# Attention and a rational feed-forward block on one core: a stored instruction order in place of a list scheduler, and six early loads on ScalarE's queue

## The chip, the core and the metric

The kernel runs on one core of a Trainium2 chip. The core has TensorE (PE in the profile), VectorE (DVE), ScalarE (ACT), GpSimd (POOL) and SyncE (SP), each with its own queue of instructions that it works through in order; they meet through semaphores. Loads and stores are issued on the queue of an engine (SPq or ACTq in the profile when they are) and carried out by 16 DMA engines. The metric is the device time of one execution in microseconds.

## The reference, cut to what matters

```python
q, k, v: (8, 8, 576, 64);  p: (8, 8, 32, 64);  w_in: (512, 2048);  w_out: (2048, 512);  a: (4,);  b: (2,)

def sm_attn(qq, kk, vv):
    s = scale * qq @ kk.T                   # scale = 1 / 8
    s = exp(s - max(s, -1))
    return (s / (sum(s, -1) + 1e-9)) @ vv

pp  = sm_attn(p, k, v)                      # 32 packed rows for each head
att = sm_attn(q, pp, pp)                    # 576 x 64 for each head
x = att.transpose(0, 2, 1, 3).reshape(4608, 512)
h = x @ w_in
P = a[0] + a[1]*h + a[2]*h**2 + a[3]*h**3
Q = 1 + abs(b[0])*abs(h) + abs(b[1])*h**2
out = (P / (Q + 1e-6)) @ w_out
```

The two weight matrices arrive as 64-bit floats, 8 MB each, and are turned into 32-bit floats on the chip, in integer arithmetic.

## The kernel before

**Work.** The eight batches go one after another. For each there is a generator `attention(bb)` (L614), then sixteen *units* (two halves of 288 tokens by eight chunks of 256 hidden columns). A unit is `hidden` (L880): TensorE forms h in PSUM (tile `h`), ScalarE and VectorE form the rational function from it (`Y`, `U`, `sq`, `V`), and the result becomes the tile `gh` (and `gl`, its rest). Three units later `acc_block` (L963) multiplies it by w_out into the tiles `acc`. `m_chunk` (L852) multiplies packed values by a chunk of w_in, which gives the tile `m` that `hidden` uses as weights. `remainder` (L932) does the last 64 tokens of two batches together (`at<-w,half` in the profile). The first batch is computed in plain 32-bit matmuls, with twelve of its units also plain in the second product; all later work splits each operand in two parts of shorter mantissa (`gh`/`gl`, `AH`/`AL`) and multiplies three of the four pairs.

**Start.** Before the first unit, q, k, v and p of batch 0 have to arrive, attention of batch 0 has to run, and weights have to be converted: `convert` (L495) takes a *word* (1 MB as it comes from memory), with two ScalarE operations and three on VectorE, the last of them on GpSimd for every second word. There are sixteen words. `constants` (L401) forms scaled copies of `a` and `b` and a square root of |b[1]| from `b`: a chain of twelve small VectorE operations and two on ScalarE (`Ln`, `Exp`), and four `reg_load`s that put results into ScalarE's registers, which the first `hidden` needs.

**Order.** The whole kernel is first recorded: `Planner` (L31) keeps 6793 entries (engine, operation, operands), a tiled group of matmuls being one entry. `edges` (L157) finds what must precede what. `schedule` (L192) is a list scheduler with a table of costs and latencies; `order` (L250) runs it forward and backward in turn, 5 slacks by 6 rounds, and keeps the best. The first 26 entries (loads for the start, and one GpSimd copy) are pinned: they come first on their queues in program order. `issue` (L281) then emits all entries in the order found, so each engine's queue is fixed. `idle` (L1075) puts short matmuls with a zero operand (`zero`) in front of a TensorE entry where the planner's times leave it a gap of at least 180 ns within the first 150 us.

The start's loads are recorded at L1006 to L1011, all on SyncE: two words, the last 64 rows of k (`AH<-in_k`), a third word, p (`pn`, four loads of 16 KB), k, rows of q, a fourth word, v, a fifth word and q; then in `constants` the four numbers `a` and the two numbers `b`, each broadcast over 128 partitions (`ab`).

Of the kernel before, what the change touches and what calls it, by code (L numbers as in the profile page):

```python
# [23 lines left out]
P = 128  # L24
# [4 lines left out]
S = 2.0**-40  # L29


class Planner:
# [27 lines left out]
    ROUNDS = 6  # L60
    SWITCH = 95
    SLACK = 60, 100, 150, 220, 300
# [5 lines left out]
    def __init__(self, nc):  # L68
        self.nc, self.ops, self.pinned = nc, [], 0
# [122 lines left out]
    def schedule(self, before, after, rank, back=0):  # L192

        n = len(rank)
        need = [len(x) for x in before]
        at, start, end = [0.0] * n, [0.0] * n, [0.0] * n
        soon = {e: [] for e in self.ENGINES}
        ready = {e: [] for e in self.ENGINES}
        free = dict.fromkeys(self.ENGINES, 0.0) if back else dict(self.FIRST)
        port = {"vector": 0.0, "gpsimd": 0.0}  # L200
        mode, landed, dma = None, [], 0.0
        for i in range(n):
            if not need[i]:
                heapq.heappush(soon[self.ops[i][0]], (0.0, rank[i], i))
        now = 0.0
        left = n
        while left:
            for e in self.ENGINES:
                while soon[e] and soon[e][0][0] <= now:
                    heapq.heappush(ready[e], heapq.heappop(soon[e])[1:])  # L210
                if free[e] > now or not ready[e]:
                    continue
                if e == "sync" and not back and len(landed) >= self.IN_FLIGHT and landed[-self.IN_FLIGHT] > now:
                    free[e] = landed[-self.IN_FLIGHT]
                    continue
                _, i = heapq.heappop(ready[e])
                left -= 1
                s = now
                if e == "tensor" and not back and self.modes[i] != mode:
                    s += self.SWITCH  # L220
                    mode = self.modes[i]
                if not back and self.shared[i]:
                    s = max(s, port["vector" if e == "gpsimd" else "gpsimd"])
                    port[e] = s + self.costs[i]
                start[i] = s
                end[i] = free[e] = s + self.costs[i]
                if e == "sync":
                    if back:
                        dma = max(dma, end[i]) + self.transfers[i]
                        end[i] = dma + self.DMA_START + self.DMA_END - self.DMA_ISSUE  # L230
                    else:
                        dma = max(dma, s + self.DMA_START) + self.transfers[i]
                        end[i] = dma + self.DMA_END
                        landed.append(end[i])
                for j in after[i]:
                    need[j] -= 1
                    f = self.ops[j][0]
                    way = self.WAY.get((f, e) if back else (e, f), self.PASS)
                    way += back * (way > 0)
                    at[j] = max(at[j], end[i] + way)  # L240
                    if not need[j]:
                        heapq.heappush(soon[f], (at[j], rank[j], j))
            now = min(
                t
                for e in self.ENGINES
                for t in ([free[e]] if ready[e] else [max(soon[e][0][0], free[e])] if soon[e] else [1e12])
            )
        return start, end

    def order(self):  # L250
# [7 lines left out]
        for i, x in enumerate(before):  # L258
            for j in x:
                after[j].append(i)  # L260
# [863 lines left out]
```

## Time and profile before

| what | value |
|---|---|
| three timed runs | 774.97, 776.93, 778.88 us; median 776.93 |
| the profiled execution's own time | 776.27 us |
| its span, first to last instruction | 774.5 us |
| mean granted TensorE clock | 0.990 |
| busy: PE, DVE, ACT, POOL | 740.3, 687.1, 653.0, 473.2 us |
| moved by DMA | 56.0 MB, of which 19.9 MB in the first 60 us |

The profile is of one execution, 1.8 us longer than its span and 0.66 us below the median of the timed runs. Busy times of TensorE come from modelled ends of pipelined matmuls. The profile names lines of the recorder: nearly every operation has line L291, so groups are told apart by their tiles (`h<-AH,m` is the output tile, then the inputs).

### The profile page before, as it was taken

How to read it: one execution, taken by the hardware profiler on the slowest of the kernel's cores; microseconds unless marked ns; L12 is line 12 of the kernel's file. 1: busy time of each engine (PE TensorE's matmuls, PEld its weight loads, DVE VectorE, ACT ScalarE, POOL GpSimd, SP SyncE). 2: the span in 40 equal slices, each digit the busy share in tenths (PEclk: the TensorE clock that was granted, in tenths of full speed). 3: DMA queues.
4: the chain of work that ended last, by engine and by line, in shares of the span. 5: the costliest groups of instructions: out<-in, count | busy, mean ns of one | idle time of the engine just before them, and what ended most of it. 6: DMA issues, size and time to landing. Idle time of an engine off the chain costs nothing.

```text
span 774.5 us, 14987 instructions
## 1 busy us (share of the span) xinstructions
PE 740.3 (96%) x5332; PEld 568.4 (73%) x5332; DVE 687.1 (89%) x1289; ACT 653.0 (84%) x1465; POOL 473.2 (61%) x456
## 2 busy tenths in 40 slices
PE   2779999999999999999999999999999999999997
PEld 2445554588778887778788887778788887868885
DVE  4899999998999889998999889998999889998863
ACT  5789988999887898889886898989887898898872
POOL 1143568876695557756686556755686556866663
PEclk9879999999999999999999999999999999999999
DMA  9992630204601155023701155023701141000001
GB/s 299 338 372 76 193 41 0 85 29 55 104 1 56 44 68 91 1 87 48 111 1 55 45 55 104 2 86 41 117 1 55 42 57 35 1 2 28 28 0 41
DMA packets 152171, 56.03 MB, mean 72 GB/s; under 512 B 122272, under 2 KB 141472, under 8 KB 152096
## 3 DMA queue, kind: packets, MB, share of 16 engines
q1 hardware_dynamic: 151856, 54.81, 31.0%
q8 instruction: 42, 0.69, 0.4%
q14 instruction: 33, 0.27, 0.1%
q10 hardware_dynamic: 240, 0.26, 0.1%
HBM read 45.62 MB, written 9.44 MB: 71 GB/s over the span
## 4 chain that ended last, share of the span: by engine, by line
PE 68%; DVE 16%; DMA 7%; ACT 4%; issue 2%; POOL 2%; SPq 1%; ACTq 0%; DVEq 0%; POOLq 0%
PE acc L291 35%; PE h L291 20%; PE at L291 12%; DVE Y L291 8%; DMA w<-in_moe_w_in_dram 2%; DMA m<-in_moe_w_in_dram 2%; DVE V L291 2%; DVE kx L291 2%; DVE m L291 2%; DVE small L291 2%; DMA w<-in_q_dram 1%; SPq L291 1%; ACT Y L291 1%; POOL gl L291 1%; DVE w L291 1%
## 5 line engine op out<-in xcount | busy, mean ns | idle before, releaser
L291 POOL TENSOR_TENSOR U<-U,sq 128x576 f32<-128x576 f32 x128 | 185.4, 1449 | 94.6 <-ACT sq L291 47.3
L291 PE MATMUL acc<-w,gh 128*128 128x512 f32 x736 | 235.7, 406 | 0.7 <-DVE G L291 0.4
L291 PE MATMUL h<-AH,m 128*128 128x288 f32 x1024 | 199.5, 317 | 4.0 <-DVE Y L291 3.5
L291 PEld LDWEIGHTS h<-AH,m 128*128 128x128 f32 x1024 | 161.2, 189 | 46.5 <-DVE Y L291 24.5
L291 POOL TENSOR_TENSOR gl<-Y,gh 128x512 fp32r<-128x512 f32 x116 | 150.3, 1296 | 45.0 <-ACT gh L291 22.8
L291 PEld LDWEIGHTS acc<-w,gh 128*128 128x128 f32 x736 | 132.6, 188 | 38.7 <-issue 9.1
L291 ACT ACTIVATE Y<-h,abS 128x288 f32<-128x288 f32 x256 | 127.5, 513 | 30.5 <-PE h L291 26.2
L291 PE MATMUL acc<-w,gl 128*128 128x512 f32 x384 | 149.3, 413 | 0.0
L291 DVE SCALAR_TENSOR_TENSOR Y<-Y,abS,V 128x576 f32<-128x576 f32 x128 | 103.2, 806 | 35.2 <-ACT V L291 34.9
L291 ACT ACTIVATE sq<-h 128x288 f32<-128x288 f32 x256 | 108.4, 425 | 29.0 <-PE h L291 15.7
L291 DVE TENSOR_TENSOR Y<-Y,h 128x288 f32<-128x288 f32 x256 | 111.0, 448 | 20.6 <-ACT U L291 7.6
L291 DVE SCALAR_TENSOR_TENSOR Y<-Y,abS,h 128x288 f32<-128x288 f32 x256 | 125.7, 507 | 2.2
L291 ACT ACTIVATE U<-h 128x288 f32<-128x288 f32 x256 | 101.9, 426 | 8.0 <-DVE V L291 7.0
L291 ACT ACTIVATE V<-U,one 128x576 f32<-128x576 f32 x128 | 98.7, 771 | 8.0 <-DVE Y L291 3.8
L291 DVE SCALAR_TENSOR_TENSOR V<-U,V 128x576 f32<-128x576 f32 x128 | 96.4, 753 | 0.0
L291 PE MATMUL h<-AL,m 128*128 128x288 f32 x448 | 96.3, 295 | 0.0
L291 DVE SCALAR_TENSOR_TENSOR Y<-V,Y 128x576 f32<-128x576 f32 x116 | 87.1, 751 | 1.4
L291 PEld LDWEIGHTS acc<-w,gl 128*128 128x128 f32 x384 | 71.8, 188 | 20.7 <-issue 6.8
L291 ACT ACTIVATE V<-V 128x576 f32<-128x576 f32 x128 | 85.0, 664 | 0.8
L291 ACT CAST gh<-Y 128x512 fp32r<-128x512 f32 x116 | 74.1, 638 | 7.4 <-DVE Y L291 6.9
L291 PE MATMUL acc<-half,gh 128*128 128x512 f32 x240 | 80.0, 411 | 0.0
L291 POOL COPY G<-Y 128x64 f32<-128x64 f32 x116 | 27.5, 237 | 76.7 <-DVE Y L291 70.5
(139 smaller groups left out, 1007.5 us busy)
## 6 DMA issues: line engine op xcount, KB each, us to landing
w<-in_moe_w_out_dram SPq DMA_DIRECT2D x16, 512.0 KB, 6.6
out_dram<-half SPq DMA_DIRECT2D x15, 512.0 KB, 3.0
nat<-in_k_dram SPq DMA_DIRECT2D x48, 144.0 KB, 3.8
nat<-in_q_dram SPq DMA_DIRECT2D x48, 144.0 KB, 4.3
nat<-in_v_dram SPq DMA_DIRECT2D x24, 256.0 KB, 3.4
m<-in_moe_w_in_dram SPq DMA_DIRECT2D x10, 512.0 KB, 6.9
w<-in_moe_w_in_dram SPq DMA_DIRECT2D x6, 512.0 KB, 8.7
nat<-in_k_dram SPq DMA_DIRECT2D x4, 512.0 KB, 6.4
```

The costliest lines, as they stand in the source:

```text
L291: getattr(getattr(self.nc, engine), name)(*args, **kwargs)
```

## The change

**The order.** The list scheduler and its rounds go. In their place stands a text of about 8,000 characters, `ORDER`, which unpacks to 6793 numbers, one for each recorded entry. `replay` walks through that order once with the old costs, only to get start times, which `idle` still uses.

```diff
-        after = [[] for _ in range(n)]
-        for i, x in enumerate(before):
-            for j in x:
-                after[j].append(i)
-        first = self.schedule(before, after, list(range(n)))
-        best = None
-        for slack in self.SLACK:
-            start, end = first
-            for r in range(self.ROUNDS):
-                s, e = self.schedule(after, before, [-x for x in end], slack)
...
+        low, high = np.frombuffer(zlib.decompress(base64.b85decode(ORDER)), np.uint8).reshape(2, -1).astype(int)
+        order = (np.cumsum(low + 256 * high) % 2**16).tolist()
+        place = {i: r for r, i in enumerate(order)}
+        assert sorted(order) == list(range(n)), "the order is of another program"
+        assert all(place[j] < place[i] for i in range(n) for j in before[i]), "the order breaks a dependence"
+        self.start, self.end = self.replay(order, before)
...
+    def replay(self, order, before):
+
+        start, end = [0.0] * len(order), [0.0] * len(order)
+        free, port = dict(self.FIRST), {"vector": 0.0, "gpsimd": 0.0}
+        mode, landed, dma = None, [], 0.0
+        for i in order:
+            e = self.ops[i][0]
+            s = max([free[e]] + [end[j] + self.WAY.get((self.ops[j][0], e), self.PASS) for j in before[i]])
...
+            start[i], end[i] = s, s + self.costs[i]
+            free[e] = end[i]
```

**The early loads.** `b`, the four loads of batch 0's p, and `a` move from SyncE's queue to ScalarE's and are recorded first. The GpSimd copy of p is recorded after all loads of the start. Nothing is pinned any more.

```diff
-        nc.sync.dma_start(ab[:, 0:4], a.rearrange("(o n) -> o n", o=1).broadcast_to([P, 4]))
-        nc.sync.dma_start(ab[:, 4:6], b.rearrange("(o n) -> o n", o=1).broadcast_to([P, 2]))
...
-                nc.sync.dma_start(pn[32 * j : 32 * j + 32, :, 0, :], src)
-            nc.gpsimd.tensor_copy(pn[:, :, 1, :], pn[:, :, 0, :])
+                (nc.sync if bb else nc.scalar).dma_start(pn[32 * j : 32 * j + 32, :, 0, :], src)
+            if bb:
+                nc.gpsimd.tensor_copy(pn[:, :, 1, :], pn[:, :, 0, :])
...
-    for what in (2, "r", 3, "p", "k0", "k1", "qr", 4, "rv", "v0", "v1", 5, "q0", "q1"):
+    nc.scalar.dma_start(ab[:, 4:6], b.rearrange("(o n) -> o n", o=1).broadcast_to([P, 2]))
+    load(0, "p")
+    nc.scalar.dma_start(ab[:, 0:4], a.rearrange("(o n) -> o n", o=1).broadcast_to([P, 4]))
+    for what in (2, "r", 3, "k0", "k1", "qr", 4, "rv", "v0", "v1", 5, "q0", "q1"):
...
-    nc.pin()
+    nc.gpsimd.tensor_copy(NAT[0, "p"][:, :, 1, :], NAT[0, "p"][:, :, 0, :])
```

**What the table says.** Unpacked with the two lines of `order`, and each number named by the entry that the code records under it, the table's queues begin like this (`w` is half a word of weights):

```
SP before:  w w w w, k rows, w w, p p p p, k k, q rows x2, w w, v rows x2, v v, w w, q q, b, a, ...
SP after:   w w w w, w w, k rows,          k k, q rows x2, w w, v rows x2, v v, w w, q q,       ...
ACT before: 6 operations of three words, 4 copies of kx, small, kx, 2 of a fourth word, ...
ACT after:  b, p p p p, a, reg_load x3, Ln, Exp, reg_load, 6 operations of three words, 4 copies of kx, small, kx, ...
DVE before: one, zero, 8 operations of three words, ...     (the 12 small ones of constants at places 29 to 53, counted from 0)
DVE after:  one, zero, the 12 small ones, 8 operations of three words, ...
```

On TensorE the first 69 entries, through the products of `win` for three chunks, are the same but for the place of a few transposes; after that the order differs throughout, though entries stay near their old places (on average 7.5 places away among 3352). The old order runs through `h` and `acc` in blocks of 2 to 12; the new one mixes them: it changes from `h` to `acc` or back 834 times, where the old one does so 310 times. Changes between tiled groups of small matmuls and whole ones are 146, before 152. Early on ScalarE's queue, the copies of `m` for the second chunk (entries 240 and 241) now come ahead of the conversion of the word in `w2` (272 and 273), where they came after it; the copies of `m` for the third chunk (280, 281) and the copy of `small` (328) also come earlier, by a few places each.

More of the change, by code (lines that the diff above doesn't have):

```diff
@@ L1 @@
-import heapq
-from collections import deque
+import base64
+import zlib
 from contextlib import ExitStack
@@ L190, in edges @@
         return edges
[L192 to L200, printed above, removed]
-        mode, landed, dma = None, [], 0.0
[L202 to L247, printed above, removed]
@@ new lines, in replay @@
+    def replay(self, order, before):
+        start, end = [0.0] * len(order), [0.0] * len(order)
+        free, port = dict(self.FIRST), {"vector": 0.0, "gpsimd": 0.0}
+        mode, landed, dma = None, [], 0.0
+        for i in order:
+            e = self.ops[i][0]
+            s = max([free[e]] + [end[j] + self.WAY.get((self.ops[j][0], e), self.PASS) for j in before[i]])
+            if e == "sync" and len(landed) >= self.IN_FLIGHT:
+                s = max(s, landed[-self.IN_FLIGHT])
+            if e == "tensor" and self.modes[i] != mode:
+                s, mode = s + self.SWITCH, self.modes[i]
+            if self.shared[i]:
+                s = max(s, port["vector" if e == "gpsimd" else "gpsimd"])
+                port[e] = s + self.costs[i]
+            start[i], end[i] = s, s + self.costs[i]
+            free[e] = end[i]
+            if e == "sync":
+                dma = max(dma, s + self.DMA_START) + self.transfers[i]
+                end[i] = dma + self.DMA_END
+                landed.append(end[i])
@@ L256, in order @@
         before = self.edges()
-        after = [[] for _ in range(n)]
-        for i, x in enumerate(before):
-            for j in x:
-                after[j].append(i)
-        first = self.schedule(before, after, list(range(n)))
-        best = None
-        for slack in self.SLACK:
-            start, end = first
-            for r in range(self.ROUNDS):
-                s, e = self.schedule(after, before, [-x for x in end], slack)
-                m = max(e)
-                rank = [m - x for x in e]
-                rank[: self.pinned] = range(-self.pinned, 0)
-                start, end = self.schedule(before, after, rank)
-                if best is None or max(end) < best[0]:
-                    best = self.best = max(end), start, end
-        self.end, self.start = best[0], best[1]
-        self.deps, self.t0 = dict(enumerate(before)), best[1]
-        return sorted(range(n), key=lambda i: (best[1][i], i))
-    def pin(self):
-        self.pinned = len(self.ops)
+        low, high = np.frombuffer(zlib.decompress(base64.b85decode(ORDER)), np.uint8).reshape(2, -1).astype(int)
[4 more added lines that the diff above has]
+        self.start, self.end = self.replay(order, before)
+        self.deps, self.t0, self.best = dict(enumerate(before)), self.start, (max(self.end), self.start, self.end)
+        return order
     def issue(self, idle):
```

103 lines of the change are left out of this document (100 added, 3 removed).

## The prediction

> **What bounds the kernel now.** I read the page first, then the busy time by stretches, then TensorE's waits.
>
> ```profile
> span 774.5 us, 14987 instructions
> PE 740.3 (96%) x5332; PEld 568.4 (73%) x5332; DVE 687.1 (89%) x1289; ACT 653.0 (84%) x1465; POOL 473.2 (61%) x456
> PE   2779999999999999999999999999999999999997
> DMA  9992630204601155023701155023701141000001
> ```
>
> TensorE is busy nearly everywhere except in the first three of 40 slices, and just there the DMA engines are at 9 tenths or more. The stretches, with TensorE's busy time first, then its weight loads, VectorE, ScalarE, GpSimd:
>
> ```profile
> 0.00:20.00 20.00, 4.97 (x22) 4.42 (x22) 9.72 (x10) 10.32 (x12) 3.36 (x8) 1.00 0.97 297
> 20.00:40.00 20.00, 15.19 (x244) 8.69 (x242) 16.99 (x45) 15.53 (x35) 2.43 (x1) 0.87 1.08 343
> 40.00:60.00 20.00, 15.31 (x87) 9.57 (x88) 17.39 (x28) 16.83 (x34) 8.32 (x5) 0.79 1.02 354
> 60.00:80.00 20.00, 20.00 (x167) 11.25 (x166) 19.96 (x41) 19.89 (x45) 7.73 (x5) 1.00 0.17 55
> 80.00:100.00 20.00, 19.34 (x95) 10.26 (x95) 19.77 (x37) 19.99 (x40) 14.62 (x7) 1.00 0.70 195
> 400.00:500.00 100.00, 99.84 (x750) 79.44 (x748) 90.66 (x173) 86.00 (x198) 66.42 (x66) 1.00 0.28 50
> ```
>
> From 0 to 60 us TensorE is idle for 15.03 + 4.81 + 4.69 = 24.5 us, from a span of which it is idle 34.2 (774.5 - 740.3). From 60 to 100 us TensorE, VectorE and ScalarE are full at once, and in the middle of the kernel TensorE idles 0.16 us in 100. So another order can win in the first 60 us, a little in the stretch after it, and hardly anything in the middle of the kernel unless the matmuls themselves run closer together. TensorE's waits say the same:
>
> ```profile
> PE at L291 <- DMA nat<-in_k_dram: 15.0, 1, 15.0
> PE at L291 <- ACT m L291: 4.3, 4, 1.6
> PE h L291 <- DVE Y L291: 3.5, 4, 1.8
> PE at L291 <- ACT small L291: 2.1, 1, 2.1
> ```
>
> All the waits that it names and that are over 2 us are here; the first three columns after the colon are the sum, the count and the longest.
>
> **Part 1, p and the constants leave SyncE's queue.**
>
> ```profile
> 4.74 3.40 SPq L291 DMA_DIRECT2D pn<-in_p_dram  x4
> 9.56 1.30 SPq L291 DMA_DIRECT2D nat<-in_k_dram  x2
> ab<-in_moe_b_dram SPq DMA_DIRECT2D x1, 1.0 KB, 8.8
> pn<-in_p_dram SPq DMA_DIRECT2D x4, 16.0 KB, 7.6
> out_dram<-full ACTq DMA_DIRECT2D x2, 64.0 KB, 2.5
> ```
>
> (The last three: KB each and us from issue to landing; p's is that of the first 24 us.) SyncE can issue k up to 4.8 us earlier (9.56 - 4.74). But k is queued behind six loads of 512 KB and one of 128 KB, 3.3 MB, and the stretch to 20 us has its DMA engines 0.97 busy at 297 GB/s: 3.3 MB take 11 us at that rate whenever they are issued. What goes away ahead of k is p's own 64 KB, 0.2 us at 297 GB/s, and p must still be moved by the same engines beside it. I take **-0.2**; bounds 0 and -4.8 (the whole earlier issue). The constants' two loads stood behind q and held nothing that the path waits for.
>
> **Part 2, the same six loads at the head of ScalarE's queue.** This is the price of the change. Behind them the table puts three `reg_load`s, `Ln`, `Exp` and a fourth `reg_load`, all of which need `a` or `b` landed and the small VectorE chain done; and behind these stand the six conversions of the first three words and then the copies of `kx` that attention needs. What waits for a late ScalarE is therefore all of attention.
>
> ```profile
> 0.73 1.28 ACT L365 ACT_TABLE_LOAD   x1 [0.73 <-PEq L1109]
> 5.87 1.10 ACT L291 ACTIVATE m<-m 128x1024 f32<-128x1024 f32 x1 [3.85 <-DMA m<-in_moe_w_in_dram]
> 6.87 1.10 ACT L291 ACTIVATE win<-m 128x1024 int32<-128x1024 uint32 x1
> 14.29 1.12 ACT L291 ACTIVATE win<-m 128x1024 int32<-128x1024 uint32 x1
> 16.09 0.59 ACT L291 COPY kx<-at 128x512 f32<-128x512 f32 x1 [0.67 <-PE at L291]
> 37.41 0.27 DVE L291 TENSOR_SCALAR root<-root 128x1 f32<-128x1 f32 x1
> 37.88 0.21 ACT L291 ACTIVATE root<-root 128x1 f32<-128x1 f32 x1
> 769.37 0.85 ACTq L291 DMA_DIRECT2D out_dram<-full  x2
> ```
>
> Two issues on ScalarE's queue took 0.85 us, so six take 2.6; the table load ends at 2.01, the sixth, `a`, starts at 4.1. No row shows a load on ScalarE's queue beside a full SyncE queue. Nearest is a store there at 2.5 us; as far up as it goes is `b`'s 8.8 us in the full queue; as far down, the shortest landing of p in this run:
>
> ```profile
> DMA to landing us min/median/max: 1.5/1.8/8.6
> ```
>
> So `a` lands between 5.6 and 12.9 us; with 2.5 us, at 6.6. The chain behind it is about 1.5 us of work after `b`'s part (rows in part 3) and four passages between engines; `Ln` (37.88) started 0.2 us after the end of the VectorE operation that it waits for, so I estimate 2.3 us. The first conversion then starts at 8.9 (7.9 to 15.2) in place of 5.87. Six conversions at one per 1.00 us (5.87 to 6.87) with a last of 1.12 take 6.1, ending at 15.0 (14.0 to 21.3), where the first copy of `kx` started at 16.09. At 15.0 the delay is covered, because the six took from 5.87 to 15.41 before, 3.4 us more than they need; at 21.3 attention starts 5.2 us late. I take **+0.5**, between 0 and **+5.2**, near the store's row.
>
> The Trainium skill (DMA: Bandwidth & Descriptors, "Queues, rings and completion order") says that each DMA engine goes round-robin between the queues that have work, packet by packet, so these small loads would not stand behind SyncE's backlog; by it they land near 1.5 us, the term is 0 and the sum 0.5 us lower. No run here shows it yet. The same page ("Issuing engines are not separate DMA queues") says that a second issuing engine saves issue time only; the trace, with its DMA engines 0.97 busy, agrees, as in part 1.
>
> **Part 3, the constants' chain leaves VectorE's busy stretch.**
>
> ```profile
> L291 DVE TENSOR_SCALAR root<-root x5: 113/146/267, 32.4 to 37.4; 128x1 int32<-128x1 int32 x3, 128x1 f32<-128x1 f32 x2
> L291 DVE RECIPROCAL root<-root x2: 156/156/156, 36.6 to 38.9; 128x1 f32<-128x1 f32 x2
> L291 ACT ACTIVATE root<-root x2: 213/214/216, 37.9 to 38.2; 128x1 f32<-128x1 f32 x2
> L291 DVE SCALAR_TENSOR_TENSOR root<-root x1: 214/214/214, 39.1 to 39.1; 128x1 f32<-128x1 f32 x1
> ```
>
> Five at about 0.146, two at 0.156 and one of 0.214 make 1.26; the other four (`root` from `ab`, three writes of `abS`) are as small, about 0.15 each: 1.9 us in all. They stood between 31 and 40 us, ahead of the first `h`. In the first 20 us VectorE is idle for 10.3 (20 - 9.72), so there they cost nothing unless `a` is late as in part 2. **-1.9**; bounds 0 (if TensorE then waits for something else) and -2.3 with ScalarE's two.
>
> **Part 4, the reordering from 40 to 60 us.** ScalarE's copies of `m` and `small` move ahead of word conversions: these are the waits of 4.3 and 2.1 us above. What is late next is VectorE or ScalarE themselves, which have 20 - 17.39 = 2.6 and 20 - 16.83 = 3.2 us to give in that stretch. So at most 6.4, and I take the smaller of the two, **-2.6**; bounds 0 and -6.4.
>
> **Part 5, the rest.** Two things are left on TensorE after 60 us: short matmuls that fill planned gaps, and waits of `h` for `Y` (3.5 us, above).
>
> ```profile
> L288 PE MATMUL acc<-w,zero 128*64 128x96 f32 x14 | 2.2, 264 | 0.0
> L288 PE MATMUL acc<-half,zero 128*64 128x96 f32 x6 | 0.7, 254 | 0.0
> ```
>
> Fillers are 2.9 us busy, in a stretch where VectorE is full too: **-1.0**, bounds 0 and -2.9. Of the waits, **-2.0**, bounds 0 and -3.5. The finer mixing of `h` and `acc` itself I cost at nothing, from the chain of waits:
>
> ```profile
> 149.13 1.85 PE h L291 x12
> 160.84 1.58 PE h L291 x12
> 162.42 2.09 PE acc L291 x9
> ```
>
> The 12 matmuls of `h` end at 162.42 and the 9 of `acc` start there: going from one to the other took no time. What covers it is that both operands have long been ready; the first row, 0.27 us longer for the same 12, shows a block whose cover was thin.
>
> **Sum.** -0.2 + 0.5 - 1.9 - 2.6 - 1.0 - 2.0 = **-7.2 us**. The profiled execution took 776.27 (span 774.5 and 1.8 around it), so 769.1; it lies 0.66 below the median of 776.93, so **769.7**. With all bounds at once on the good side (-4.8 + 0 - 2.3 - 6.4 - 2.9 - 3.5 = -19.9) it is 757; on the bad side (+5.2) 782.
>
> **Rivals.**
>
> *Mixing brings waits (slower).* TensorE takes its entries in order. In blocks of 6 and 12, a late operand holds up work that depends on the same operand anyway; with 834 changes between `h` and `acc` instead of 310, an `acc` whose `gl` is late holds up an `h` that was ready, and ScalarE and VectorE behind that. One wait of this kind costs 3.5 / 4 = 0.9 us (the row of `h` waiting for `Y`). Eight more than before undo the sum; if 17 of the 524 added changes, one in 30, meet one, that is +15 - 7.2: **784.7**. For it: TensorE has only 0.16 us per 100 of idle time in the middle, so any new wait there is a loss in full. Against it: VectorE and ScalarE have 9 and 14 us of idle time per 100 there to catch up.
>
> *Nothing gained (same).* The loads set the start: DMA is full to 60 us, SyncE issues the same loads in nearly the same order, and by 60 us TensorE has done what the weights' arrival allows. Then parts 3 and 4 only move idle time, part 5's 3 us remain or go into small new waits: between **774 and 777**. For it: three full slices of DMA. Against it: TensorE's waits in 40 to 60 us name ScalarE, not DMA.
>
> *Far more (faster).* The new order keeps TensorE fed through 20 to 60 us, where it idles 4.81 + 4.69 = 9.5 us, and wins part 3's 1.9 and all of part 5's 6.4 too: -17.8 and a little back, about **761**. For it: TensorE ran at a granted clock of 0.79 there, which fewer gaps would raise. Against it: VectorE and ScalarE have only 2.6 and 3.2 to give.
>
> *Late constants (not faster).* Part 2 at its upper bound, +5.2 in place of +0.5: -2.5, so **774.4**. It needs `a` to land 8.8 us after issue.
>
> **Chances.** Forecast 0.48, mixing 0.15, nothing 0.15, late constants 0.07, far more 0.15. 0.5% of 776.93 is 3.9 us, about what a measurement of this kernel can tell from no change: faster is below 773.0, slower above 780.8. Four fifths of the forecast and all of "far more" give 0.54 faster, some of the rest 0.02; of mixing, 0.13 lies above 780.8, and 0.03 of the others; 0.28 is left for the same. The range is 759 to 782: down to "far more", up to part 2's bound, leaving out most of mixing (0.12) and a little below.
>
> **What would show it.** The marks on TensorE before:
>
> ```profile
> 14.96 1.09 PE L291 MATMUL at<-ident,nat 128*128 128x128 f32 x4 [14.96 <-DMA nat<-in_k_dram]
> 42.58 2.29 PE L291 MATMUL h<-AH,m 128*128 128x288 f32 x4 [0.23 <-DVE AH L291]
> ```
>
> Part 1: TensorE's first transposes of k within 0.5 us of 14.96. Part 2: ScalarE's first conversion near 8.9, the first copy of `kx` by 16.6; wrong if conversions start after 11. Part 3: no `root` rows after 20 us, the first `h` about 2 us before its 42.6. Part 4: TensorE's waits for ScalarE's `m` and `small` together below 4 us, its busy time in 40 to 60 us near 18. Part 5: fewer than 20 fillers and waits for `Y` near 1.5. The forecast is wrong if TensorE's idle time between 150 and 750 us grows by more than 3 us, or if its idle time to 60 us is not below 21.

## The result and the profile after

The changed kernel takes **784.41 us** (783.50 to 785.59, five runs); the kernel before, run beside it, 777.03 (774.97 to 778.88, five runs). The ratio is 1.010, with a 95% interval of 1.0085 to 1.0116: slower by 7.4 us, where 769.7 was forecast and the range ended at 782. The page of the changed kernel, its span and the slices:

```profile
span 782.2 us, 14977 instructions
...
PE   0768999999999999999999999999999999999997
DMA  8984370020531009102821107210630205000001
```

The first slice of TensorE is now empty, and the DMA engines, full in the first three slices before, are at 8, 9, 8 and then 4. The stretches, in the columns that the prediction used:

```profile
0.00:20.00 20.00, 1.17 (x6) 1.20 (x7) 3.59 (x16) 5.27 (x7) 0.99 (x7) 1.00 0.84 257
20.00:40.00 20.00, 14.82 (x188) 11.02 (x186) 17.86 (x28) 15.37 (x32) 5.71 (x3) 0.91 1.01 290
40.00:60.00 20.00, 13.76 (x132) 8.02 (x126) 17.64 (x27) 15.63 (x31) 5.74 (x3) 0.83 0.90 317
60.00:80.00 20.00, 16.98 (x95) 9.43 (x95) 18.31 (x37) 18.94 (x41) 5.72 (x5) 0.91 0.42 142
150.00:750.00 600.00, 598.10 (x4383) 475.60 (x4382) 551.09 (x1030) 521.66 (x1194) 397.56 (x399) 1.00 0.26 49
```

And the last of these stretches in the kernel before:

```profile
150.00:750.00 600.00, 596.23 (x4364) 482.62 (x4363) 543.85 (x1027) 519.08 (x1196) 390.70 (x393) 1.00 0.26 48
```

To 60 us TensorE idles 18.83 + 5.18 + 6.24 = 30.25 us, 5.7 more than before, and from 60 to 80 another 3.02 where it was full. From 150 to 750 us it idles less than before (1.90 against 3.77). Most of the loss lies at the start, and ScalarE's queue shows what happens there:

```profile
0.77 0.42 ACTq L340 DMA_DIRECT2D ab<-in_moe_b_dram  x1
1.22 5.48 ACTq L340 DMA_DIRECT2D pn<-in_p_dram  x4
8.50 0.35 ACTq L340 DMA_DIRECT2D ab<-in_moe_a_dram  x1
14.83 0.44 ACT L340 ACTIVATE root<-root 128x1 f32<-128x1 f32 x2 [12.81 <-DVE root L340]
16.42 1.10 ACT L340 ACTIVATE m<-m 128x1024 f32<-128x1024 f32 x1 [1.15 <-DVE abS L340]
22.60 0.64 ACT L340 COPY kx<-acc 128x512 f32<-128x512 f32 x1
```

`a`, the sixth load, is issued at 8.50 us. `Ln` and `Exp` (the row of `root`) wait until 14.83, and only at 16.42, not at 5.87, does the first word's conversion begin; the first copy of `kx` follows at 22.60 in place of 16.09. The chain of waits, followed back from that conversion (start, length, what):

```profile
1.22 7.26 DMA pn<-in_p_dram
8.50 5.12 DMA ab<-in_moe_a_dram
13.65 0.17 DVE abS L340
```

The issue of `a` waits until the first load of p has landed, 7.26 us after that one's issue; then `a` itself takes 5.12 us; then the small operations and register loads pass between VectorE and ScalarE for 2.8. The first of these waits comes from semaphores: in the trace every load, whichever queue issued it, lands on one of eight completion semaphores. `a`, issued at 8.50, has that of p's first load, which landed at 8.48; p's fourth load, issued at 6.38, has that of `b`, which landed at 6.36. Each was issued only when the load before it on its semaphore had landed. From issue to landing in the first 24 us (KB each, us):

```profile
pn<-in_p_dram ACTq DMA_DIRECT2D x4, 16.0 KB, 7.7
ab<-in_moe_b_dram ACTq DMA_DIRECT2D x1, 1.0 KB, 5.6
ab<-in_moe_a_dram ACTq DMA_DIRECT2D x1, 2.0 KB, 5.1
```

TensorE's two marks, the first transposes of k and the first `h`, which stood at 14.96 and 42.58:

```profile
18.83 1.09 PE L340 MATMUL acc<-ident,nat 128*128 128x128 f32 x4 [18.83 <-DMA nat<-in_k_dram]
49.33 2.29 PE L340 MATMUL h<-AH,m 128*128 128x288 f32 x4 [1.86 <-DVE AH L340]
```

The first `h` is 6.75 us late, the end of the span 7.7. So two things went wrong in the first 20 us: ScalarE stood still for the constants, and the words and k themselves came later. Which of them costs what, and what the table does by itself, only further kernels could tell.

### The profile page after: what moved, and what is told of

It is laid out like the page before. It is cut to its first block, busy times and chain, and to the rows that moved or that the text cites. A ratio compares the mean times of both kernels' runs of the same rounds, so it can differ in the third digit from the quotient of the medians.

```text
span 782.2 us, 14977 instructions
## 1 busy us (share of the span) xinstructions
PE 742.4 (95%) x5329; PEld 566.5 (72%) x5329; DVE 693.6 (89%) x1289; ACT 654.9 (84%) x1465; POOL 471.3 (60%) x456
## 4 chain that ended last, share of the span: by engine, by line
PE 86%; ACT 6%; DVE 4%; DMA 3%; issue 1%; SPq 1%; POOL 1%; ACTq 0%; DVEq 0%; POOLq 0%
PE acc L340 44%; PE h L340 26%; PE at L340 15%; DMA pn<-in_p_dram 2%; DVE Y L340 1%; ACT V L340 1%; DVE w L340 1%; ACT kx L340 1%; ACT Y L340 1%; DMA ab<-in_moe_a_dram 1%; ACT sq L340 1%; ACT m L340 1%; SPq L340 1%; ACT U L340 0%; ACT win L340 0%
## 5 line engine op out<-in xcount | busy, mean ns | idle before, releaser
L340 PE MATMUL acc<-w,gh 128*128 128x512 f32 x736 | 254.2, 408 | 1.2 <-ACT half L340 0.7
L340 PE MATMUL h<-AH,m 128*128 128x288 f32 x1024 | 234.4, 319 | 5.4 <-DVE Y L340 3.2
L340 PEld LDWEIGHTS h<-AH,m 128*128 128x128 f32 x1024 | 177.6, 190 | 50.1 <-DVE Y L340 17.8
L340 ACT ACTIVATE Y<-h,abS 128x288 f32<-128x288 f32 x256 | 129.6, 513 | 20.8 <-PE h L340 19.4
L340 DVE SCALAR_TENSOR_TENSOR Y<-Y,abS,h 128x288 f32<-128x288 f32 x256 | 128.1, 509 | 4.0
L340 ACT ACTIVATE sq<-h 128x288 f32<-128x288 f32 x256 | 106.3, 419 | 17.7 <-PE h L340 11.6
L340 ACT ACTIVATE U<-h 128x288 f32<-128x288 f32 x256 | 104.7, 420 | 12.8 <-PE h L340 9.1
L340 PE MATMUL h<-AL,m 128*128 128x288 f32 x448 | 105.3, 297 | 0.0
L340 PE MATMUL acc<-half,gh 128*128 128x512 f32 x240 | 86.3, 415 | 0.0
L340 ACT CAST gh<-Y 128x512 fp32r<-128x512 f32 x116 | 73.3, 632 | 14.6 <-DVE Y L340 11.9
L340 PEld LDWEIGHTS h<-AL,m 128*128 128x128 f32 x448 | 76.6, 188 | 6.8 <-issue 1.3
```

What stands on the lines that cost most here:

```text
L340: getattr(getattr(self.nc, engine), name)(*args, **kwargs)
```

## The experiments

Edits of order are shown as the beginnings of queues in the notation of the section on the change (`w` is half a word). In kernels marked "own order" the list scheduler's order of the kernel before is kept as a fixed table and only the entries shown are moved. Each time is given with its ratio to the kernel before run beside it, and the 95% interval. A kernel that ran only once, for its profile, has a single time, which the spread of the kernel before (some 5 us from lowest to highest) makes worth little; there the marks of its profile count. The marks are the start of ScalarE's first conversion of a word, of TensorE's first transposes of k, and of the first `h`. They vary too: where the start is that of the kernel before (before, list_then_table, list_tail), k lies between 14.16 and 14.96 and the first `h` between 41.56 and 42.58, and where it is the table's with the loads at their old places (table_only, table_then_list) k is at 15.93 and 14.30, the first `h` at 43.74 and 42.29. A difference of 1 to 1.5 us between two marks says little.

### The change taken apart

**table_only.** The new table, with the loads back on SyncE and the constants' arithmetic at its old places.

```diff
 SP:  w w w w, w w, k rows,
+     p p p p,
      k k, q rows x2, w w, v rows x2, v v, w w, q q,
+     b, a, ...
-ACT: b, p p p p, a, reg_load x3, Ln, Exp, reg_load, 6 operations of three words, ...
+ACT: 6 operations of three words, ...
-DVE: one, zero, the 12 small ones, 8 operations of three words, ...
+DVE: one, zero, 8 operations of three words, ...
```

> The new table, but the six early loads back on SyncE's queue at their old places and the chain of the constants back at its old places on VectorE and ScalarE. Theory 1 (the early loads and what waits for them cost the time, the order elsewhere is worth little): TensorE's first transposes of k near 15 us, ScalarE's first conversion near 5.9, the first h within 1.5 us of 42.6, the time 770 to 778. Theory 2 (the finer mixing of h and acc costs the time): the start is as early as that, but the time stays at 781 or above, because the loss comes after 60 us.

Measured: 777.99 us, 1.0026 (1.0008 to 1.0044); first conversion 5.92, transposes of k 15.93, first `h` 43.74. The table alone loses 2 us and wins nothing; the other 5 come with the early loads and the arithmetic that waits for them.

**loads_only.** The list scheduler again, with the six loads on ScalarE's queue, pinned first.

```diff
-        nc.sync.dma_start(ab[:, 0:4], ...)
-        nc.sync.dma_start(ab[:, 4:6], ...)
+    nc.scalar.dma_start(ab[:, 4:6], ...)
+    load(0, "p")
+    nc.scalar.dma_start(ab[:, 0:4], ...)
```

> The old list scheduler, with the six early loads on ScalarE's queue, pinned first there as in the changed kernel; the constants' chain stands where the list scheduler puts it. Theory 1: the loads themselves are half of the loss: the first transposes of k come near 18.8 us in place of 15.0, a lands near 13.6, the first h 2 to 4 us later than 42.6, the time 778 to 782. Theory 2: the time stays within 2 us of 777.

Measured: 785.23 us, 1.0123 (1.0088 to 1.0157); first conversion 16.25, k 19.52, first `h` 49.60. The list scheduler, too, put the constants' arithmetic ahead of the words once `b` and `a` were early by its costs. So the same damage comes without the table.

**loads_sp.** The changed kernel with the six loads on SyncE's queue, ScalarE still waiting for `a`.

```diff
-    nc.scalar.dma_start(ab[:, 4:6], ...)
+    nc.sync.dma_start(ab[:, 4:6], ...)
-                (nc.sync if bb else nc.scalar).dma_start(pn[32 * j : 32 * j + 32, :, 0, :], src)
+                nc.sync.dma_start(pn[32 * j : 32 * j + 32, :, 0, :], src)
-    nc.scalar.dma_start(ab[:, 0:4], ...)
+    nc.sync.dma_start(ab[:, 0:4], ...)
```

> The changed kernel with the six early loads issued on SyncE's queue, at the places in SyncE's order that the table gives them (b and two of p behind the first four halves of words); all else as in the changed kernel, so ScalarE still waits for a before its first conversion. If two queues at once slow each other's loads: k comes near 15.5 in place of 18.8 and the first word's landing near 5.8 in place of 7.2; a lands at 9 to 11, conversions start at 12 to 13.5, the first h near 46, the time 779 to 782. If it is only that ScalarE waits and that few loads can be under way at once: k stays near 18, conversions at 15 to 16, the time 783 to 785.

Measured: 785.40 us, 1.0123 (1.0085 to 1.0161), k at 15.56 and the first `h` at 49.70. ScalarE's first conversion:

```profile
16.49 1.14 ACT L340 ACTIVATE m<-m 128x1024 f32<-128x1024 f32 x1 [1.15 <-DVE abS L340]
```

Here k is nearly on time, and the kernel is as slow: ScalarE's wait is enough by itself.

**chain_late.** The changed kernel, its loads where it has them, but ScalarE's part of the arithmetic behind the first word or later, and VectorE's two operations that need `a` behind the three words.

```diff
-ACT: b, p p p p, a, reg_load x3, Ln, Exp, reg_load, 6 operations of three words, 4 copies of kx, ...
+ACT: b, p p p p, a, 2 operations of a word, Ln, Exp, 4 operations of two words, 4 copies of kx, small, kx, reg_load x3, ...
```

> The changed kernel, but nothing that needs a stands ahead of the first conversions: Ln and Exp (which need b only) come behind the first word's two ScalarE operations, the four reg_loads behind the first copies of kx, and the two VectorE operations on abS behind the three words. Theory 1: conversions start at 7 to 9 us in place of 16.4, the first copies of kx at 19.7 to 20.5, right behind k's landing at 18.8, in place of 22.6; the first h 2 to 3 us earlier than 49.3, the time 781 to 782.5. Theory 2: 783 to 785, as the change.

Measured: 782.86 us, 1.0088 (1.0055 to 1.0120); first conversion 8.93, k 18.34, first `h` 46.81. Without the wait 3 us of the start are still lost to late words, so the loads' place has a price of its own: the kernel still loses 6.9 us to the kernel before.

### What the table costs, and where

**table_then_list** and **list_then_table.** One kernel takes the table's first 871 entries (to about 149 us) and the list's order behind them, the other the list's first 891 and the table behind.

```diff
+        early = set(order[:891])
+        order = order[:891] + [i for i in table if i not in early]
```

> The start of before (loads and constants at their old places), the table's order for its first 871 entries, up to the first split matmul of the second batch (near 150 us), and the list scheduler's order for all entries behind. If the table's finer mixing costs time in the middle of the kernel and its early part gains a little (stores of the first batch came 0.6 us earlier in the run with the table alone, although its first h was 1.2 us later): 773 to 775.5, 2 to 4 us under the table alone (778.0), one to two hundred steps of 0.1 us less between matmuls. If mixing is free: 776 to 779, as the table alone.

> The reverse: the list scheduler's order for its first 891 entries, up to the same matmul, and the table's order for all behind. If mixing costs in the middle: the first store of the first batch as before (145.2 us), two batches in the middle take 177 to 178 us in place of 175.6, and the time is 778 to 781. If mixing is free: 775 to 777.

Measured: table_then_list 784.76 us, 1.0141 (1.0119 to 1.0162), with its first `h` at 42.29 but its second store of results 7.8 us late: the table's beginning puts off work that the list's order presumes done at the seam, so this kernel says nothing of the table's start. list_then_table has no such seam: 778.12 us, 1.0037 (1.0023 to 1.0051). The first and the last store of half a batch on SyncE, in the kernel before, table_only and list_then_table:

```profile
145.25 0.62 SPq L291 DMA_DIRECT2D out_dram<-half  x1
770.69 0.41 SPq L291 DMA_DIRECT2D out_dram<-half  x1
```

```profile
144.67 0.61 SPq L382 DMA_DIRECT2D out_dram<-half  x1
774.49 0.42 SPq L382 DMA_DIRECT2D out_dram<-half  x1
```

```profile
145.32 0.62 SPq L422 DMA_DIRECT2D out_dram<-half  x1
772.79 0.41 SPq L422 DMA_DIRECT2D out_dram<-half  x1
```

From first to last are 625.44, 629.82 and 627.47 us. This difference is a steady measure (625.2 to 625.7 in eight kernels that keep the order of the kernel before from there on, 629.8 to 630.1 in six that keep the table's): in the changed kernel it is 778.77 - 148.82 = 629.95, so what is lost at the start is neither won back nor added to. (In table_only the first store is entry 827 of the order, in the list's it is 852; with it so much earlier, the 4.4 us overstate the loss.) The table's middle and end lose 2.0. TensorE's groups from 150 to 600 us, before and in list_then_table:

```profile
L291 PE MATMUL acc<-w,gh 128*128 128x512 f32 x498 | 156.4, 398 | 0.3 <-ACT half L291 0.3
L291 PE MATMUL h<-AH,m 128*128 128x288 f32 x652 | 117.5, 300 | 1.4 <-DVE Y L291 1.4
```

```profile
L422 PE MATMUL acc<-w,gh 128*128 128x512 f32 x494 | 169.0, 399 | 1.2 <-ACT half L422 0.7 <-POOL w L422 0.5
L422 PE MATMUL h<-AH,m 128*128 128x288 f32 x649 | 144.4, 303 | 0.9 <-DVE Y L422 0.6
```

In the same 450 us, with 0.3 us more idle time in the records (2.05 us against 1.74 for all groups together), a few matmuls of each kind fewer were done. So the loss sits between matmuls that the profile shows back to back. I argue from this that changing between `h` and `acc` costs a little each time; a kernel with fewer changes and otherwise the same order was not run, so it is not shown.

### The constants' arithmetic moved early, without the table

**chain_early** and **ab_act.** Own order. In the first, `b` and `a` go behind the third word on SyncE's queue and the arithmetic on them to earlier places, VectorE's among the operations of the first three words; the second issues `b` and `a` at the head of ScalarE's queue instead.

```diff
 chain_early
-SP:  w w w w, k rows, w w, p p p p, k k, ...
+SP:  w w w w, k rows, w w, b, a, p p p p, k k, ...
 ab_act
-ACT: 6 operations of three words, ...
+ACT: b, a, 6 operations of three words, ...
```

> The kernel before, but with b and a loaded behind the third word on SyncE's queue and the constants' chain in VectorE's and ScalarE's idle time: nine VectorE operations behind the second word's, Ln and Exp behind the copy of small, the last three behind the third word, reg_load behind the fourth word. No wait ahead of a conversion. If part 3 of the prediction holds (1.9 us of VectorE's busy stretch saved): the first h 1 to 2 us earlier than 42.6 and the time 774 to 775.5 beside 776. If the time is set by the loads or by ScalarE instead: the first h within 0.5 us of 42.6 and the time 775.5 to 777.

> As the run before it, with b and a at the head of ScalarE's queue instead (p stays on SyncE's). If any loads of many small pieces on a second queue slow the words of SyncE's queue: the first word lands near 7 us (first conversion in place of 5.9) and k 1 to 3 us later than 15.0. If it is p's loads that do: the first conversion at 5.9 to 6.3, k within 0.5 us of 15.0; b and a land 2 to 5 us after issue, and the time is as in the run before it.

Measured: chain_early 777.08 us, 1.0024 (1.0009 to 1.0040), its first `h` at 43.30. Its `root` operations run from 13.4 to 20.9 us, where they ran from 31.1 to 39.1 before, and the interval leaves no room for a gain. ab_act 778.96 us, 1.0055 (1.0037 to 1.0072), first conversion 9.42, k 18.89, first `h` 45.53. In this kernel nothing on ScalarE waits for `b` or `a` ahead of the words, and p is on SyncE; still the first conversion starts 3.5 us late, waiting for its word.

### Why two loads of 3 KB delay the words

The DMA engines in the first 24 us, in 40 slices of 0.6 us (tenths busy, GB/s, packets), before and in ab_act:

```profile
DMA  0009799999999999999999999999999999999999
GB/s 0 0 0 96 222 406 413 399 382 375 396 396 369 299 226 321 341 393 375 301 297 332 352 357 338 239 213 360 348 389 354 284 221 333 335 348 353 382 418 413
DMA packets 6148, 7.43 MB, mean 309 GB/s; under 512 B 1631, under 2 KB 3935, under 8 KB 6148
```

```profile
DMA  0009345986579999999999998999989799999999
GB/s 0 0 0 140 120 151 182 304 243 151 158 202 342 372 410 395 323 208 190 258 315 243 370 317 228 318 367 373 370 265 176 143 334 369 389 402 324 297 318 325
DMA packets 5726, 6.23 MB, mean 260 GB/s; under 512 B 1882, under 2 KB 3678, under 8 KB 5726
```

From 2.4 to 7.2 us the engines are at 3 to 9 tenths and move 120 to 304 GB/s, where before they moved 222 and then 375 to 413. Four kernels, all in own order, ask what it is about these loads.

**p_act** (p's four loads at the head of ScalarE's queue, nothing else), **ab_act_late** (`b` and `a` on ScalarE's queue, but behind the first word's conversions), **w_act** (half a word at the head of ScalarE's queue) and **tiny_apart** (two added loads there, with pieces as small as those of `b` and `a`, but from 256 different addresses; nothing reads what they bring).

```diff
 p_act
-ACT: 6 operations of three words, ...
+ACT: p p p p, 6 operations of three words, ...
 ab_act_late
+ACT: 2 operations of a word, b, a, 4 operations of two words, ...
 w_act
+ACT: w, 6 operations of three words, ...
 tiny_apart
+    nc.scalar.dma_start(apart[:, 2:3], w_in[0:P, 0:1])
+    nc.scalar.dma_start(apart[:, 0:2], w_in[P : 2 * P, 0:2])
```

> The kernel before with its own order held fixed; the only edit is that the first packing queries' four loads are issued from ScalarE's queue at its head instead of SyncE's. The constants a, b and their arithmetic stay where they are. Theory: small loads issued on a second queue beside the first words delay the words, whichever loads they are, so the first conversion starts near 9.4 as it did with a and b there (5.9 before), the k transposes near 18.5 (14.5 before) and the first hidden matmul near 45.5 (42.6). Rival: only a and b do it (one source address read by 128 partitions); then the conversion stays at 5.9, the transposes come at 14.3 because SyncE's queue is four issues shorter, and the first hidden matmul at 42.4.

> As the kernel with a and b at the head of ScalarE's queue, but both are issued behind the conversions of the first word half, near 8 us instead of 0.8; the constants' arithmetic where that kernel has it. Theory one, a second queue costs whenever it is used: the conversion is untouched (5.9) but the k rows, on their way from 8 to 14 us, are delayed as the words were, transposes near 17 to 18.5. Theory two, it costs only in the first microseconds: conversion 5.9, transposes 14.5 to 15, first hidden matmul 42.5 to 43.3.

> The kernel before with its own order held fixed; one edit: the first half of the second word (256 rows of 2 KB pieces) is issued at the head of ScalarE's queue, everything else on SyncE's as before. It tells a second queue by itself from small pieces. If the second queue by itself slows the first, the first conversion starts past 8.5 and the transposes near 18. If it is the small pieces, the first word only shares the rate with a transfer of half its own size: conversion 6 to 6.8, transposes 14 to 14.8, first hidden matmul within 0.7 of 42.6.

> The kernel before with its own order held fixed and two loads added at the head of ScalarE's queue, into a buffer that nothing reads: 128 pieces of 8 bytes and 128 of 16 bytes, as b and a have, but each piece from a row of its own of the word table. With a and b themselves there the first conversion came at 9.42 and 6.2 MB moved in the first 24 us, against 5.87 and 7.4 MB. If tiny pieces are the cause: conversion past 8.5, under 6.8 MB. If it is one address read 128 times: conversion 5.9 to 6.6, over 7.1 MB.

Measured, one execution each, with first conversion, k and first `h`: p_act 777.68 us, 6.39, 14.67, 43.43; ab_act_late 775.81, 5.91, 14.96, 43.74; w_act 773.22, 7.46, 14.39, 41.48; tiny_apart 775.37, 6.12, 14.49, 41.93. The DMA engines in tiny_apart:

```profile
DMA  0009699999999999999999999999999999999999
GB/s 0 0 0 123 219 349 413 391 380 403 410 389 375 310 213 276 396 393 367 314 294 340 341 362 340 225 258 341 379 396 343 281 269 338 350 352 367 405 396 410
DMA packets 6455, 7.50 MB, mean 313 GB/s; under 512 B 1920, under 2 KB 4224, under 8 KB 6455
```

So it is not the second queue, as p and the half word there do no such harm, and not the small pieces: 256 of them from different addresses leave the rate at its level. What sets `b` and `a` apart is that each is broadcast, 128 pieces read from one address. In ab_act_late the same dip (112 to 218 GB/s at 11.4 to 13.2 us) follows them to where they now are; the first half of k is past it (14.96 as before), the second half comes 1.1 us later. On SyncE's own queue the dip is there too but shorter (loads_sp: 67 GB/s in one slice at 7.8 us), and behind the first words it delays little. All nine kernels that load `b` and `a` in the first 15 us show it.

But one address is not the whole condition. In the kernel before, the same pieces were moved from 27.6 to 29.2 us, on SyncE's queue, and the engines stayed at 9 tenths (24 to 48 us, slices of 0.6 us):

```profile
DMA  9999999999999999999999999999999999999999
GB/s 410 357 360 350 355 346 295 325 343 314 222 255 334 246 382 367 353 358 346 213 266 384 369 417 347 386 377 393 397 400 410 403 406 376 386 399 379 389 393 382
```

In table_only, where they were moved from 28.1 to 31.2 us, the engines were at 5 to 8 tenths for most of that time. That the early place of these two loads makes the words late is shown; what decides when they slow the others is open, and no kernel read one address of another array. w_act's later first conversion fits a rate shared with half a word more.

### Is the wait then the whole of the rest?

**ab_behind** and **ab_behind_fixed.** The changed kernel, p left at the head of ScalarE's queue, `b` and `a` behind the first word's conversions. In the first, `Ln` and `Exp` stand right behind `a`, and the ten small VectorE operations that need only `b` and the results of `Ln` and `Exp` stand ahead of and among the words; the second has all the arithmetic at the places of the kernel before.

```diff
 both
-ACT: b, p p p p, a, reg_load x3, Ln, Exp, reg_load, 6 operations of three words, ...
 ab_behind
+ACT: p p p p, 2 operations of a word, b, a, Ln, Exp, 4 operations of two words, ...
 ab_behind_fixed
+ACT: p p p p, 2 operations of a word, b, a, 4 operations of two words, ...
-DVE: one, zero, the 12 small ones, 8 operations of three words, ...
+DVE: one, zero, 8 operations of three words, ...
```

> The changed kernel with p's loads still at the head of ScalarE's queue; b, a and the arithmetic on them are behind the conversions of the first word half on ScalarE, and on VectorE behind the words. If the place of a and b is the whole loss beyond the table's own 2.0: conversion near 6.4, k transposes near 15, first hidden matmul 43 to 44.5, time 777 to 779 (ratio 1.001 to 1.004). If moving p or the start order of the table costs as well: over 780.

> As the changed kernel, p at the head of ScalarE's queue, b and a behind the conversions of the first word half there; Ln, Exp, the register loads and VectorE's arithmetic on the constants at the places of the kernel before. If ScalarE's wait is the cause of the loss beyond the table's: second word converted near 9.5 (14.8 with Ln in front), k transposes near 16.3, first hidden matmul 43.7 to 45, time 777.5 to 780 (ratio 1.003 to 1.006). If it stays over 782, the wait is not the cause.

Measured: ab_behind 783.73 us, 1.0104 (1.0083 to 1.0124), first `h` at 48.28; ab_behind_fixed **778.47 us, 1.0048 (1.0029 to 1.0067)**, first `h` at 44.82. ScalarE, then VectorE, in ab_behind:

```profile
6.28 1.10 ACT L369 ACTIVATE m<-m 128x1024 f32<-128x1024 f32 x1 [4.27 <-DMA m<-in_moe_w_in_dram]
14.47 0.44 ACT L369 ACTIVATE root<-root 128x1 f32<-128x1 f32 x2 [6.09 <-DMA ab<-in_moe_a_dram]
14.81 1.17 ACT L369 ACTIVATE m<-m 128x1024 f32<-128x1024 f32 x1
```

```profile
13.02 0.16 DVE L369 SCALAR_TENSOR_TENSOR root<-ab 128x1 f32<-128x1 f32 x1 [11.48 <-DMA ab<-in_moe_b_dram]
14.35 0.69 DVE L369 TENSOR_SCALAR m<-m 128x1024 int32<-128x1024 int32 x1
```

And in ab_behind_fixed:

```profile
9.12 1.22 ACT L381 ACTIVATE m<-m 128x1024 f32<-128x1024 f32 x1 [0.67 <-DMA m<-in_moe_w_in_dram]
```

```profile
8.49 0.83 DVE L381 TENSOR_SCALAR m<-m 128x1024 int32<-128x1024 int32 x1 [6.96 <-ACT win L381]
```

What was expected of ab_behind overlooked that the arithmetic still waits for the constants in front of words: it held ScalarE's second word until 14.81 instead of 9.12 and VectorE's first until 14.35 instead of 8.49. The pair is the cleanest statement of the case: the same loads at the same places, and 5.3 us between them by a few operations of 0.2 us that stand in front of a wait. With these out of the way the changed kernel keeps 3.3 us of its loss, 2.1 of them the table's. The remaining 1.2 may belong to `b` and `a` being loaded while k is under way (k at 16.67 against 15.93 in table_only), but p is on ScalarE's queue here too and the two intervals overlap, so that is not shown.

### A version that beats both

**list_tail**, **w_act_timed**, **act_tail** and **act_tail_fixed.** list_tail keeps the list's order to entry 5248 (about 600 us) and has the table's behind it; w_act_timed is w_act again, in rounds. act_tail_fixed joins them. act_tail was meant to, but there the list scheduler ran with the half word on ScalarE and found another order.

```diff
+        early = set(order[:5248])
+        order = order[:5248] + [i for i in table if i not in early]
...
-                    nc.sync.dma_start(raw[:, 512 * y : 512 * (y + 1)].rearrange("p (x y) -> p x y", x=2), src)
+                    (nc.scalar if len(nc.ops) == 2 else nc.sync).dma_start(raw[:, 512 * y : 512 * (y + 1)].rearrange("p (x y) -> p x y", x=2), src)
```

> The kernel before up to entry 5248 of its own order (about 600 us), behind it the table's order; loads and constants as before. Where the table stood behind the list from 149 us on it was 6 us late at the store near 604 us and 2 us late at the end, so the stretch behind 604 us gained 4. If that gain belongs to the table's order there: span near 770.5, time near 773 (ratio 0.995 to 0.998). If it was only a delay being absorbed by waits that stand there in the list's order (0.7 us near 510, 1.8 near 680), the store near 655 us stands where it stood before, the end within 1 us of 774.5, ratio 0.999 to 1.001.

> The kernel before with its order fixed and half of the second word at the head of ScalarE's queue, now in rounds. If the early start of its one profile is the edit's: ratio 0.996 to 0.998. If it was the spread from run to run: 0.999 to 1.001.

> The kernel before with the first half of the second word issued at the head of ScalarE's queue and the table's order behind entry 5248; a, b and p stay as before. The tail alone measured 0.9985. If half a word on the second queue starts the work earlier, as its single profile had it (first hidden matmul 41.5, first store 142.3 against 42.6 and 145.3): time near 773, ratio 0.995 to 0.998. If that profile was only the early end of the spread from run to run (another run of the unchanged start had its first store at 142.0): ratio 0.998 to 0.9995, as the tail alone.

> The same fixed order up to entry 5248, the table's order behind it, half of the second word at the head of ScalarE's queue. The tail alone gave 0.9985. Sum of both: 0.9945 to 0.9975; if the half word brings nothing: 0.998 to 0.9995; over 1.003 would say that the half word and not the list's other order made the earlier joint kernel slow.

Measured: list_tail 774.64 us, 0.9985 (0.9969 to 1.0000); w_act_timed 774.49, 0.9991 (0.9978 to 1.0005), so its early single profile was spread; act_tail 779.59, 1.0053 (1.0036 to 1.0069), with a first `h` at 42.69 and then a wait of 3.6 us for `AH` ahead of the second; act_tail_fixed **772.45 us, 0.9963 (0.9949 to 0.9977)**, faster than both kernels of this case. Its first and last store:

```profile
144.85 0.62 SPq L426 DMA_DIRECT2D out_dram<-half  x1
769.22 0.38 SPq L426 DMA_DIRECT2D out_dram<-half  x1
```

They are 624.37 us apart, 1.1 less than before; list_tail has 624.10. That much is the table's tail: from 675 to 700 us TensorE idles 1.8 us in the kernel before and not at all in these two. The other half of the gain can't be told from the start's own spread (first stores lay between 142.0 and 145.3 us in kernels whose start is the same).

### All marks side by side

| kernel | first conversion | k | first `h` | us | ratio |
|---|---|---|---|---|---|
| before | 5.87 | 14.96 | 42.58 | 775.1 to 777.0 | |
| after | 16.42 | 18.83 | 49.33 | 784.4 | 1.010 |
| table_only | 5.92 | 15.93 | 43.74 | 778.0 | 1.003 |
| loads_only | 16.25 | 19.52 | 49.60 | 785.2 | 1.012 |
| loads_sp | 16.49 | 15.56 | 49.70 | 785.4 | 1.012 |
| chain_late | 8.93 | 18.34 | 46.81 | 782.9 | 1.009 |
| ab_act | 9.42 | 18.89 | 45.53 | 779.0 | 1.006 |
| ab_behind | 6.28 | 16.30 | 48.28 | 783.7 | 1.010 |
| ab_behind_fixed | 6.35 | 16.67 | 44.82 | 778.5 | 1.005 |
| act_tail_fixed | 7.60 | 14.69 | 41.79 | 772.5 | 0.996 |

## Why the prediction was wrong

**Two steps failed: the size of part 2, and the gains of parts 3 to 5.** Between the forecast change of -7.2 us and the measured +7.4 lie 14.6. Parts 1 and 2 were taken at +0.3 and came to +5.3 (5.0 of the 14.6); parts 3 to 5, with mixing at nothing, were taken at -7.5 and came to +2.1, what table_only loses (9.6; part 3 is tested by chain_early). Either miss alone would have left the time inside the range, at 774.7 or 779.3.

**Part 2.** The term was +0.5 with an upper bound of +5.2. What the prediction had seen was right: three register loads, `Ln` and `Exp` wait for the constants, all of attention stands behind them, and conversions that start after 11 us mean it is wrong. The size was not. `a` was taken to be issued at 4.1 us and was issued at 8.50, since it had to wait for an earlier load to land; this wait was not in the sum at all, though the program that the edit gives has it. From issue to landing I took 2.5 us from a store's row near the end of the kernel, where the DMA engines are at 1 tenth; it took 5.12. The chain behind it took 2.8 where 2.3 was estimated. (That the issues wait for the table load, as was assumed, was wrong too: `b` went at 0.77.) Together the conversions began at 16.42 in place of 8.9, past the upper bound of 15.2, because that bound used the late landing but not the late issue. The term measures about 5.3 us: the changed kernel loses 7.4 to the kernel before and the table by itself 2.1. The wait and the slower transfers behind it overlap and cannot be added up: with the wait taken away but the loads early the loss is 6.9 (chain_late), with the wait but k nearly on time 9.5 (loads_sp), and only with both out of the words' way 3.3 (ab_behind_fixed). So the two together cost some 4.0, and the rest of the 5.3 is not told apart. *Late constants* was the right rival, given 7 in 100, and its 774.4 still held gains that did not exist.

The Trainium skill (DMA: Bandwidth & Descriptors, "Queues, rings and completion order") has the queues served in turn, packet by packet, by which the small loads would have landed near 1.5 us and the term would be 0. The rows of after show 5.1 to 7.7 us for them; the measurement decides, and the 3.5 and 4.8 us of the loads in tiny_apart, which slowed nothing, are above 1.5 as well.

**Part 1** had k 0.2 us earlier; it came 3.9 us later. Its reasoning, that k waits for bytes and not for its issue, holds as far as one profile tells: p_act, with p off SyncE's queue, has k at 14.67 against 14.96, not 4.8 us earlier. What it left out is the rate itself, which fell while `b` and `a` were under way. The same page of the Trainium skill ("Issuing engines are not separate DMA queues") says that a second issuing engine saves issue time alone; w_act_timed, 0.9991, agrees.

**Part 3** (-1.9) did not come in chain_early: the small operations left VectorE's busy stretch, the first `h` stood at 43.30, not at 40.7, and the time was 1.0009 to 1.0040 of that before. They were busy time on an engine for which the first `h` hardly waited: its quoted row has 0.23 us of waiting for `AH`. (chain_early also has `b` and `a` early, with a dip to 97 GB/s; its k, at 14.99, is on time.)

**Part 4** (-2.6): the waits did shrink, and TensorE gained nothing. Of the changed kernel:

```profile
PE acc L340 <- ACT kx L340: 3.9, 1, 3.9
PE at L340 <- ACT m L340: 3.2, 5, 1.0
PE h L340 <- DVE Y L340: 3.2, 3, 2.7
PE h L340 <- DVE AH L340: 1.9, 1, 1.9
```

`m` went from 4.3 to 3.2 and `small` has gone, below 4 together as marked. But a wait of 1.9 for `AH` has come and that for `kx` has doubled, and table_only, where nothing delays ScalarE, has the same 2.0 for `AH`, with TensorE busy 12.35 us from 40 to 60, not 18. The wait taken away was replaced by the next, as the upper bounds of the prediction allowed and its chosen value did not.

**Part 5** (-3.0): `Y` stayed at 3.2 for 3.5, and there are 17 fillers for 20. Neither gain is there.

**Mixing at nothing.** The mark for the rival *Mixing brings waits*, over 3 us more idle time between 150 and 750 us, was not reached; idle time there fell by 1.9. The rival's 784.7 is near the result by chance, for another reason. Yet the table is not free. From the first store to the last list_then_table loses 2.0 us and list_tail wins 1.3, so some 3 go between 149 and 600 us, and no wait shows them. The prediction's statement that the middle has nothing to give "unless the matmuls themselves run closer together" had its other side left out: they can also run further apart.

## What to carry to other kernels

Before an operation is put at the head of an in-order queue, ask for the latest time at which its operand can arrive, and count in the wait of the load's own issue; an engine that is idle in a stretch is free for that operation only until the work behind it is due. A few operations of 0.2 us in front of a late operand cost 5.3 us in the pair ab_behind and ab_behind_fixed. When a busy time is to be saved, look first whether the engine that sets the end ever waited for it.

## What was not expected of the hardware

Two loads of 3 KB in all, each one small address broadcast to 128 partitions, lowered the rate of all transfers from about 400 to between 120 and 304 GB/s for some 5 us when they ran beside the first words (ab_act); pieces of the same size and number from different addresses did not (tiny_apart), and the same two loads at 27.6 to 29.2 us did not either (before). And small loads issued on an empty queue beside a full one landed 3.5 to 8.1 us after issue, not within the 1.5 to 2.5 us that the shortest rows of the kernel before suggested.
